# Layernorm, local attention and FFN on one core: when block 3's output turns, three attention pieces and the stacked left rows are issued

## The chip, the core and the metric

The kernel runs on one core of a Trainium2 chip. The metric is the device time of one execution in microseconds. A core has TensorE (PE: matmuls; PEld is the load of the stationary operand), VectorE (DVE), ScalarE (ACT), GpSimd (POOL) and SyncE (SP). Each engine works through its own list of instructions in order, and waits at an instruction until what it depends on has signalled. SP, ACT and POOL issue DMA transfers, each in its own queue; 16 DMA engines serve all queues.

## The reference

With x of 2048 rows and 576 columns:

```
xn  = layernorm(x)
q, k, v = split(xn @ wqkv)                         # 32 heads of 18
at row s, per head: logits over the 8 rows s, s-2, ..., s-14 (rows below 0 masked)
att = softmax(logits * 18**-0.5) @ v of those rows
h   = relu(xn @ w1 + b1) ** 2                      # 4608 columns
out = x + att @ wo + h @ w2 + b2
```

All data are float32.

## The kernel before

**Precision.** Each float32 operand of a matmul is split in two: a high part, which ACT writes as a rounded copy (lines 522 `w1_hi`, 556 `w2_hi`, 998 `o_hi`, 1080 `h_hi`, 1451 `operand_hi`), and a low part, the remainder, which DVE subtracts (`w1_lo`, `w2_lo`, `o_lo`, `h_lo`, `operand_lo`; all record line 128). A product is three matmuls: high by high, high by low, low by high. Names below are of the operand's tile: `w2r` is a raw tile of W2 or the output weights, `w2s` its split; `w1s` split W1; `h` split hidden rows; `q` an attention result.

**Blocks.** The 2048 rows are four blocks of 512 (b = 0 to 3). Blocks 0 and 1 go together first (s = 0), then blocks 2 and 3 (s = 1). For the first FFN matrix, two blocks and two tiles of 128 hidden columns (a pair p, 18 of them) are one 2x2 product of matrices, computed with seven products instead of eight; `ffn_pair` (673) does one pair: seven calls of `product` (691), in the order B11, T1, T2, T3, B21, B22, T4, with relu and square between.

**Left rows.** 576 is 4 times 128 plus 64. The last 64 columns of x and rows of W1 are handled in two ways. In pairs 0 to 2 (`PLAIN` is 3) they are two extra matmuls (`left`, 700). From pair 3 on the seven combinations of these rows are stacked: `ST` holds them for x (`stk` in DRAM, loaded by `load_stack`, 633, into two tiles named `w1r`: places 0 to 3 and 4 to 6, each by two DMAs of 64 partitions), `LW` for W1 (`lw` in DRAM, loaded per pair by `load_left_weights`, 655, into a tile `st`, `mb`, or two tiles `x40`, `x41`, in turn). Then each of the seven products has one more matmul, line 698 with `w1r` as its input.

**Where these loads stand.** `part(i)` (706) is called in each pair after the second product (i = 0), after the sixth (i = 1) and after the seventh (i = 2). In s = 1 it issued, all on SP's queue: at pair 1, i = 0, both `load_stack` (four DMAs); at pair 2, i = 0, `load_left_weights` for pairs 3 and 4; later one pair's `load_left_weights` two pairs ahead. In s = 1 the split W1 of each pair comes back from DRAM in two halves by `w1_again` (535), on ACT's queue, one pair ahead; the half k = 1 holds the slots of B21, B22, T4 and, below pair 3, of the left rows. SP's queue also holds the W2 loads (line 551, issued by `w2_lo`), the stores of finished hidden rows (777) and of operands for the block products (766, 769).

**Attention.** A work item `attention(b, g)` (394) is a generator of 19 pieces for one block and one group of 8 heads, nearly all DVE work: for four row sets a product and a reduction (8 pieces), maximum and subtraction, the exponent (on ACT), normalization, and for four row sets a product and a sum (8 pieces). The last piece stores the result by eight POOL DMAs (line 434). `side(n)` runs the next n pieces; strings of digits say how many at which place.

**The last stages.** After the pairs of s = 1 come the block products for half of the hidden tiles (`phase_blocks`, 1504): 28 steps k, matmuls on line 1514, 12 or 16 to a step; after each step the splits of the operands for step k + 2, weights by the list `WHEN`, and `side(int(LAST[k]))`. Then `phase_b1` (1597) adds the other hidden tiles of block 3: 18 tiles m, 14 matmuls each (line 590), each with one `w2_hi` and `w2_lo` (for the tile two ahead), on even m also an `h_hi` and `h_lo`, and `side(int(SINGLES[m]))`. At m = 12 the attention of block 3 must be complete; `regroup` (982) gathers its rows from DRAM into `st` and `r4` (POOL, line 994). From them `o_hi` turns one column group c of 128 (DVE transpose, line 1011) and splits it (ACT, line 1012), and `o_lo` makes the low part. These stood at m = 14 to 17 for c = 0 to 3 and inside the projection for c = 4. The projection is the loop over five column groups c (`o_ops`) at the end of `phase_b1`; `tail` follows. ACT and DVE keep the order of the code, so what stands behind an `o_hi` waits with it.

Of the kernel before, what the change touches and what calls it, by code (L numbers as in the profile page):

```python
# [9 lines left out]
F32R = mybir.dt.float32r  # L10
# [6 lines left out]
P = 128  # L17
S, D, F = 2048, 576, 4608
H, DH, W, DIL = 32, 18, 8, 2
TB = 512  # L20
NB = S // TB
NJ = TB // P
NC = 5
NF = F // P
NP = NF // 2
# [18 lines left out]
PLAIN = 3  # L44
# [1 line left out]
PIECES = (0, 0, 0, 2, 3, 4, 0, 3, 2, 0, 2, 2, 1, 0, 2, 2, 4, 5)  # L46
SPOTS = ('000001',) + ('110022', '110023', '110023', '110023') * 4 + ('110021',)
QUADS = ('01111110111110', '10100010101011', '00110111111111', '10010000111111', '00000000000001', '00110010101010')
LAST = '0000000000000000001111111111'
SINGLES = '12121212121200000000'  # L50
PAIRED = tuple(range(1, 16, 2))
SINGLE = tuple(p for p in range(NP) if p not in PAIRED)
# [7 lines left out]
def block_kernel(ctx: ExitStack, tc: tile.TileContext, x, xt, wqkv, wo, w1, b1, w2, b2, w1l, w2q, w2l, out):  # L60
# [3 lines left out]
    sb = ctx.enter_context(tc.tile_pool(name="sb", bufs=1))  # L64
# [62 lines left out]
    def tt(out, a, b, op):  # L127
        return nc.vector.tensor_tensor(out=out, in0=a, in1=b, op=op)  # L128
# [18 lines left out]
    def four(dt=F32):  # L147
        return sb.tile([P, 2, TB], dt, name="r4", bufs=4)
# [23 lines left out]
    def load_two_rows(b, h):  # L172
        rows_of.setdefault(b, {})
        t = sb.tile([P, 2, D], F32, name="st")
        for j in range(2):
            rows_of[b][2 * h + j] = t[:, j:j + 1]
        nc.gpsimd.dma_start(t, xv[b, :, 2 * h:2 * h + 2])
# [422 lines left out]
    def dims(t, off, *ap):  # L600
        a = t[tuple(slice(0, 1) for _ in t.shape)]
        return bass.AP(tensor=a.tensor, offset=a.offset + off, ap=[*ap])
# [16 lines left out]
    def left_x(s):  # L619
        v = rv.pop(s)  # L620
        x = lambda k: v[:, STACK[k]]
        tt(x(T3), x(B11), x(T1), ALU.subtract)
        tt(x(T1), x(T1), x(T4), ALU.add)
        tt(x(T2), x(T1), x(B11), ALU.subtract)
        tt(x(B22), x(B21), x(T2), ALU.subtract)

        def store(k, part):
            for i in range(NS):
                nc.gpsimd.dma_start(dims(stscr[s], k * NS * TB + i * TB, [2 * NS * TB, L], [1, TB]), part[:, i])

        yield from high_low(v, store)

    def load_stack(s, t, i):
        n = min(t.shape[1], NS - i)
        for h in range(2):
            nc.sync.dma_start(t[2 * h * L:2 * (h + 1) * L, :n].bitcast(F32), stscr[s][:, i:i + n])
        for k, place in STACK.items():
            if i <= place < i + n:
                ST[k] = t[:, place - i]

    def load_left_w(i, v):
        rv["w", i] = v
        nc.sync.dma_start(v[:, :4], w1l[i])
# [11 lines left out]
    def load_left_weights(s, p):  # L655
        place = (p - PLAIN) % 2 + 1 if not s else (p - PLAIN) % 3
        tiles = ([sb.tile([P, 2 * NS * P], F32R, name="st")[:, :NS * P].rearrange("p (s c) -> p s c", c=P)] if place == 0 else
                 [sb.tile([P, NS, P], F32R, name="mb")] if place == 1 else
                 [mt.tile([P, 4, P], F32R, name="x40"), mt.tile([P, 4, P], F32R, name="x41")])
        i = 0  # L660
        for t in tiles:
            n = min(t.shape[1], NS - i)
            nc.sync.dma_start(t[:, :n].rearrange("p s c -> p (s c)").bitcast(F32),
                              dims(lwscr[p // G], p % G * 2 * L * NS * P + i * P, [NS * P, 2 * L], [0, 2], [1, n * P]))
            for k, place in STACK.items():
                if i <= place < i + n:
                    LW[p % 3, k] = t[:, place - i]
            i += n
# [4 lines left out]
    def ffn_pair(s, p, work, first=False):  # L673
# [32 lines left out]
        def part(i):  # L706

            if not s and (p, i) in ROWS:
                b, h = ROWS[p, i]
                if h:  # L710
                    next(rv["m", b])
                else:
                    rv["m", b] = statistics(b)
                if h < 2:
                    load_two_rows(b, h)
            if i == 0 and not s and p + 1 >= PLAIN and not last:
                load_left_weights(s, p + 1)
            if i == 0 and s:
                for q in range(PLAIN if p + 1 == PLAIN else p + 2, min(p + 3, NP) if p + 1 >= PLAIN else 0):
                    load_left_weights(s, q)  # L720
            if i == 0 and p == 1 and s:
                for q in (0, 4):
                    load_stack(1, sb.tile([P, 4, TB], F32R, name="w1r", bufs=2), q)
            if i == 2 and p == PLAIN - 1 and not s:
                load_stack(0, mt.tile([P, 1, TB], F32R, name="x4d"), 6)
            if s:
                return
            if (p, i) == (0, 1):
                rv["x of"] = left_x(0)
            if (p, i) in ((0, 1), (1, 0)):  # L730
                for _ in range(1 + p):
                    next(rv["x of"])
            if (p, i) == (1, 2):
                load_stack(0, sb.tile([P, 5, TB], F32R, name="kv", bufs=3), 0)
                load_stack(0, sb.tile([P, 1, TB], F32R, name="xf"), 5)
            r = p // G + 1
            if i == 1 and p % G == 1 and G * r < NP:
                load_left_w(r, sb.tile([P, 2 * NS, P], F32, name="st"))
            elif p % G == 2 and G * r < NP:
                if i == 0:  # L740
                    rv["of", r] = left_w(r)
                next(rv["of", r])
# [255 lines left out]
    def o_hi(b, c):  # L998
        if c == NC - 1 and b == 1:
            ot[b, c // 2] = sb.tile([P, 1, 1, TB], F32R, name="xf")  # L1000
        elif c % 2 == 0:
            ot[b, c // 2] = mt.tile([P, 2, 2, TB], F32R, name="h" if b == 1 else "w1s", bufs=3)
        hi = ot[b, c // 2][:, c % 2, 0]
        if c < NC - 1:
            if b != 1:
                of[b, c] = four()[:, 0]
            elif c % 2 == 0:
                t = four()
                of[b, c], of[b, c + 1] = t[:, 0], t[:, 1]
            src = ob[b, 0][:, :, c * L:(c + 1) * L] if c < 3 else ob[b, 1][:, :, :L]  # L1010
            nc.vector.transpose(of[b, c].rearrange("p (u f) -> p u f", f=L), src)
            nc.scalar.activation(hi, of[b, c], AF.Copy)
            return
        t = of[b, c] = four()
        n = L // 2
        nc.vector.transpose(t[:, 0].rearrange("p (u k f) -> p u k f", k=2, f=n),
                            ob[b, 1][:, :, None, OB - n:].to_broadcast([P, NJ * G, 2, n]))
        nc.scalar.activation(t[:, 1].bitcast(F32R), t[:, 0], AF.Copy)

    def o_lo(b, c):  # L1020
        hi = ot[b, c // 2][:, c % 2, 0]
        t = of.pop((b, c))
        if c < NC - 1:
            tt(ot[b, c // 2][:, c % 2, 1], t, hi.bitcast(F32), ALU.subtract)
            return
        nc.vector.tensor_scalar(out=t[:, 0], in0=t[:, 0], scalar1=flip[:, 0:1], scalar2=None, op0=ALU.mult)
        nc.vector.scalar_tensor_tensor(out=hi, in0=t[:, 1], scalar=flip[:, 1:2], in1=t[:, 0],
                                       op0=ALU.mult, op1=ALU.add)
# [475 lines left out]
    def phase_blocks():  # L1504
# [28 lines left out]
        for k in range(len(ORDER)):  # L1533
# [54 lines left out]
            if k == 25:  # L1588
                load_h(1, SINGLE[1])
                h_hi(1, SINGLE[0])  # L1590
                h_lo(1, SINGLE[0])
            side(int(LAST[k]))
        load_h(1, SINGLE[2])
# [3 lines left out]
    def phase_b1():  # L1597
        b = 3
        phase_blocks()
        m = 0  # L1600
        for j, p in enumerate(SINGLE[:-1]):
            for f in range(2):
                w2_hi()
                if f == 0:
                    h_hi(1, SINGLE[j + 1])
                add(b, tile_products(b, 2 * p + f, hs[1, p]))
                w2_lo()
                if f == 0:
                    h_lo(1, SINGLE[j + 1])
                elif j + 3 < len(SINGLE):  # L1610
                    load_h(1, SINGLE[j + 3])
                if len(xr[b]) < 2 and (m == 12 or not queue and current[0] is None):
                    complete(b)
                    regroup(b, 0)
                    regroup(b, 1)
                    open_left(b)
                    load_left(b)
                for c in {14: (0,), 15: (1,), 16: (2,), 17: (3,)}.get(m, ()):
                    o_hi(b, c)
                    o_lo(b, c)  # L1620
                side(int(SINGLES[m]))
                m += 1
        for c in range(NC):
            w2_hi()
            add(b, o_ops(b, c), (NC - 2,) if c == NC - 1 else ())
            w2_lo()
            if c == 1:
                o_hi(b, NC - 1)
                o_lo(b, NC - 1)
        tail()  # L1630

    def tail():
# [396 lines left out]
    phase_a(0, filler)  # L2029
    phase_a(1, phase_b0())  # L2030
    phase_b1()


# [58 lines left out]
```

## Time and profile before

| | us |
|---|---|
| median of 3 runs | 1110.2 |
| lowest, highest | 1109.54, 1112.1 |
| the profiled execution | 1111.5 |
| its span, first to last instruction | 1109.8 |
| PE idle inside the span (1109.8 - 1088.1) | 21.7 |

The times are of whole executions. The profile is one other execution, and its own time lies 1.7 us above its span. "Busy" is time in which an engine had an instruction in work; matmuls overlap, so a busy PE may still run slowly when the granted clock (PEclk, 1.00 is full) is low. "Chain" is the order of work that ended last, followed back from the end. A row such as `x14 [5.61 <-ACT w2s L562]` says that 14 instructions of a kind follow one another, and that their engine was idle for 5.61 us before, until ACT's work on `w2s` at line 562 ended. Times in rows are counted from the span's start. `SPq` and `ACTq` are DMA issues in the queues of SP and ACT.

### The profile page before, as it was taken

The page shows a single profiled execution, that of the slowest core. Times are in us where ns is not written, and L with a number is a line of the kernel's source. Part 1 is how long each engine was busy: PE and PEld are TensorE (multiplying, and loading weights), DVE is VectorE, ACT ScalarE, POOL GpSimd, SP SyncE. Part 2 cuts the span into 40 slices and gives each one's busy share as a digit, 9 for nine tenths or more (in the row PEclk, how much of TensorE's full clock was granted, in tenths as well). Part 3 has the DMA queues.
Part 4 walks back from the last instruction along what each step waited for, and adds up shares of the span by engine and source line. Part 5 has one row for each costly group of instructions (what it writes and reads, how often), then busy time and mean ns, then how long its engine had stood idle before and what let it go on. Part 6 is the DMA issues. An engine that isn't in the chain of part 4 may idle for free.

```text
span 1109.8 us, 13933 instructions
## 1 busy us (share of the span) xinstructions
PE 1088.1 (98%) x4871; PEld 911.2 (82%) x4871; DVE 931.4 (84%) x1245; ACT 570.9 (51%) x800; POOL 160.3 (14%) x294
## 2 busy tenths in 40 slices
PE   9999999999999999999999998999999999999978
PEld 7998888888888888888899877888788788887867
DVE  7967899999998979989998676879789887878955
ACT  5556665666566554555353443555554565533422
POOL 5011220212130100012012201112012030000010
PEclk9999999999999999999999998999999999999999
DMA  8759997898897797876866989998798897664752
GB/s 285 250 196 319 301 394 279 312 372 281 319 340 295 247 370 259 276 240 237 300 184 208 391 252 336 341 376 317 300 384 312 328 348 245 210 200 137 251 178 92
DMA packets 106886, 312.53 MB, mean 282 GB/s; under 512 B 12864, under 2 KB 39488, under 8 KB 95168
## 3 DMA queue, kind: packets, MB, share of 16 engines
q1 hardware_dynamic: 70048, 198.75, 50.9%
q0 software_dynamic: 15584, 71.96, 17.8%
q10 hardware_dynamic: 21184, 40.94, 10.9%
q8 instruction: 38, 0.62, 0.2%
q14 instruction: 32, 0.26, 0.1%
HBM read 216.62 MB, written 94.98 MB: 281 GB/s over the span
## 4 chain that ended last, share of the span: by engine, by line
PE 80%; DVE 10%; DMA 5%; issue 3%; ACT 1%; POOL 0%; SPq 0%; ACTq 0%; DVEq 0%; POOLq 0%
PE p L698 32%; PE p L590 29%; PE p L1187 7%; PE p L1514 6%; DVE pr L128 4%; PE p L1843 2%; DVE h L128 2%; PE p L1191 1%; DMA w1s<-w 1%; DVE w2s L128 1%; PE p L1898 1%; DMA op<-h 1%; PE p L704 1%; DMA out<-h 1%; PE p L1753 1%
## 5 line engine op out<-in xcount | busy, mean ns | idle before, releaser
L590 PE MATMUL p<-h,w2s 128*128 128x512 f32 x1618 | 392.6, 392 | 5.6 <-ACT w2s L562 5.6
L590 PEld LDWEIGHTS p<-h,w2s 128*128 128x128 f32 x1618 | 305.8, 189 | 71.2 <-ACT w2s L562 6.0
L698 PE MATMUL p<-X,w1s 128*128 128x512 f32 x864 | 219.9, 390 | 1.5 <-DVE r L128 1.5
L698 PEld LDWEIGHTS p<-X,w1s 128*128 128x128 f32 x864 | 162.4, 188 | 36.0 <-DVE r L128 1.9
L698 PE MATMUL p<-S,w1s 128*128 128x512 f32 x648 | 167.3, 394 | 0.9 <-ACT p L786 0.9
L698 PEld LDWEIGHTS p<-S,w1s 128*128 128x128 f32 x648 | 121.0, 189 | 30.0 <-ACT r L806 2.9
L562 ACT ACTIVATE w2s<-w2r 128x640 fp32r<-128x640 f32 x132 | 96.7, 734 | 87.9 <-PE p L590 61.8
L434 POOL DMA_DIRECT2D o<-q x128 | 69.5, 620 | 471.6 <-DVE q L128 471.1
L128 DVE TENSOR_TENSOR w2s<-w2r,w2s 128x576 fp32r<-128x576 f32 (+1 forms) x133 | 99.7, 750 | 15.5 <-ACT w2s L562 15.5
L745 ACT ACTIVATE r<-r,b1t 128x512 f32<-128x512 f32 x72 | 52.1, 724 | 116.4 <-DVE r L128 113.6
L128 DVE TENSOR_TENSOR h<-h 128x1024 fp32r<-128x1024 f32 (+1 forms) x74 | 72.6, 989 | 23.2 <-ACT h L762 13.7
L128 DVE TENSOR_TENSOR pr<-lg,kv 128x1152 f32<-128x1152 f32 x64 | 86.7, 1355 | 1.3
L128 DVE TENSOR_TENSOR pr<-q,kv 128x1152 f32<-128x1152 f32 x64 | 86.7, 1354 | 1.1
L128 DVE TENSOR_TENSOR r<-p,r 128x512 f32<-128x512 f32 (+2 forms) x81 | 55.0, 681 | 38.4 <-ACT r L831 20.3
L405 DVE TENSOR_REDUCE lg<-pr 128x64 f32<-128x1152 f32 x64 | 86.4, 1350 | 1.0
L128 DVE TENSOR_TENSOR pr<-pr 128x576 f32<-128x576 f32 (+1 forms) x128 | 77.5, 606 | 3.1
L753 ACT ACTIVATE r<-r 128x1024 f32<-128x1024 f32 x56 | 59.2, 1057 | 0.9
L806 ACT ACTIVATE r<-p 128x512 f32<-128x512 f32 x36 | 21.6, 599 | 57.2 <-PE p L698 57.1
L128 DVE TENSOR_TENSOR w1s<-w1r,w1s 128x1024 fp32r<-128x1024 f32 (+2 forms) x42 | 46.2, 1102 | 5.6 <-ACT w1s L523 5.0
L831 ACT ACTIVATE r<-p 128x512 f32<-128x512 f32 x36 | 21.6, 600 | 56.4 <-PE p L698 56.4
L745 ACT ACTIVATE r<-p,b1t 128x512 f32<-128x512 f32 x72 | 48.2, 671 | 0.0
L128 DVE TENSOR_TENSOR h<-r,h 128x1024 fp32r<-128x1024 f32 (+2 forms) x35 | 39.9, 1146 | 7.6 <-ACT r L753 6.0
(263 smaller groups left out, 1489.8 us busy)
## 6 DMA issues: line engine op xcount, KB each, us to landing
kv<-kvq POOLq DMA_DIRECT2D x32, 1296.0 KB, 9.3
w2r<-in_w SPq DMA_DIRECT2D x112, 320.0 KB, 4.5
w<-w1s SPq DMA_DIRECT2D x21, 1024.0 KB, 7.6
w1s<-w ACTq DMA_DIRECT2D x19, 1024.0 KB, 8.2
h<-r SPq DMA_DIRECT2D x28, 512.0 KB, 6.2
h<-h SPq DMA_DIRECT2D x28, 512.0 KB, 4.3
w<-w1s SPq DMA_DIRECT2D x15, 768.0 KB, 9.1
w1s<-w ACTq DMA_DIRECT2D x15, 768.0 KB, 7.0
```

The costliest lines, as they stand in the source:

```text
L128: return nc.vector.tensor_tensor(out=out, in0=a, in1=b, op=op)
L405: nc.vector.tensor_reduce(out=lg[:, j * HG:(j + 1) * HG].rearrange("p a w -> p w a"), in_=pr.rearrange("p w (a d) -> p w a d", d=DH), axis ...
L434: nc.gpsimd.dma_start(rows[:, i], q[i * L:(i + 1) * L, :, a:z])
L562: nc.scalar.activation(w2s[stream[i]][:, :DE], raw2[i], AF.Copy)
L590: nc.tensor.matmul(yp[b][c], v, a, start=c not in yb[b], stop=c in last and c not in [o[0] for o in ops[i + 1:]], skip_group_check=True)
L698: nc.tensor.matmul(to, l, r, start=start and i == 0, stop=i == len(mm) - 1, skip_group_check=True)
L745: nc.scalar.activation(to, a, AF.Relu, bias=b1t[:, f:f + 1])
L753: nc.scalar.activation(r, r, AF.Square)
L806: nc.scalar.activation(u[:, 0], bb, AF.Copy)
L1187: nc.tensor.matmul(to, l[:, js], r, start=start and n == 0, stop=n == len(mm) - 1, skip_group_check=True)
L1514: nc.tensor.matmul(p, l, r, start=id(p) not in begun, stop=stop, skip_group_check=True)
L1843: nc.tensor.matmul(p[:, :QW], l, r, start=k == 0, stop=k == len(mm) - 1)
```

## The change

It has three parts. The digits of `LAST` place attention pieces at steps 13, 14 and 15 of the block products, none at 19 and 21, and one each at 18, 20 and 22 to 27: eleven pieces, before ten at 18 to 27. The left rows' loads of s = 1 are divided: the first half of the stacked x rows is loaded at pair 1, i = 1, the second half at pair 2, i = 0; the left weights for pair 3 at pair 2, i = 0, those for pair 4 at pair 2, i = 2. And block 3's turns for c = 0 and 1 stand at m = 16 and 17, those for c = 2, 3 and 4 in the projection, behind products 0, 1 and 2.

```diff
-LAST = '0000000000000000001111111111'
+LAST = '0000000000000111001010111111'
...
-            if i == 0 and s:
-                for q in range(PLAIN if p + 1 == PLAIN else p + 2, min(p + 3, NP) if p + 1 >= PLAIN else 0):
-                    load_left_weights(s, q)
-            if i == 0 and p == 1 and s:
-                for q in (0, 4):
-                    load_stack(1, sb.tile([P, 4, TB], F32R, name="w1r", bufs=2), q)
+            if i == 0 and s and p + 1 == PLAIN:
+                load_left_weights(s, PLAIN)
+            if i == (2 if p + 1 == PLAIN else 0) and s and PLAIN <= p + 1 and p + 2 < NP:
+                load_left_weights(s, p + 2)
+            if i == 2 - p and p in (1, 2) and s:
+                load_stack(1, sb.tile([P, 4, TB], F32R, name="w1r", bufs=2), 4 * p - 4)
...
-                for c in {14: (0,), 15: (1,), 16: (2,), 17: (3,)}.get(m, ()):
+                for c in {16: (0,), 17: (1,)}.get(m, ()):
                     o_hi(b, c)
                     o_lo(b, c)
...
-            if c == 1:
-                o_hi(b, NC - 1)
-                o_lo(b, NC - 1)
+            if c < 3:
+                o_hi(b, c + 2)
+                o_lo(b, c + 2)
```

## The prediction

> **What bounds the kernel now.** I read the page first, then the waits of PE, the chain of waits, the windows, and the timelines of three places. The page says that PE is the bound and has little left to give:
>
> ```profile
> PE 1088.1 (98%) x4871; PEld 911.2 (82%) x4871; DVE 931.4 (84%) x1245; ACT 570.9 (51%) x800; POOL 160.3 (14%) x294
> ```
>
> The waits of PE (engine and line, what it waited for, total us, times, longest) name all of it. These are five of eight rows:
>
> ```profile
> PE p L590 <- ACT w2s L562: 5.6, 1, 5.6
> PE p L704 <- DMA w1s<-w: 5.5, 1, 5.5
> PE p L698 <- DVE r L128: 1.5, 1, 1.5
> PE p L1514 <- DVE h L128: 1.4, 1, 1.4
> PE p L1514 <- DVE w1s L128: 0.8, 2, 0.4
> ```
>
> Two waits carry 11.1 us, and the change stands at both. The first is in pair 2 of blocks 2 and 3 (s=1). The chain of waits there (start, us, what):
>
> ```profile
> 646.05 8.40 DMA out<-h
> ...
> 654.53 14.67 DMA w1s<-w
> ...
> 669.24 1.22 PE p L704 x2
> 670.46 1.71 PE p L590 x4
> 672.17 4.12 PE p L698 x12
> ...
> 676.75 1.59 PE p L590 x7
> ```
>
> PE wanted the second half of pair 2's W1 at 669.24 - 5.5 = 663.74 and had it at 669.20. A wait of this length costs more than itself: the last row is 1.59/7 = 0.227 us a matmul, while the 2 + 4 + 12 matmuls that come first took 672.17 + 4.12 - 669.24 = 7.05 us in place of 4.09. The granted clock shows why:
>
> ```profile
> 670.00:672.00 2.00, 2.00 (x7) 1.52 (x6) 0.00 (x0) 0.00 (x0) 0.00 (x0) 0.50 1.00 398
> ```
>
> So this place costs 5.5 + 2.96 = 8.5 us. The second is at block 3's output projection:
>
> ```profile
> 1064.10 0.31 DVE L128 TENSOR_TENSOR q<-pr 128x144 f32<-128x144 f32 x1
> 1064.69 4.33 POOL L434 DMA_DIRECT2D o<-q  x8 [35.66 <-DVE q L128]
> 1072.44 0.56 POOL L994 DMA_DIRECT2D st<-o  x1 [3.42 <-DMA o<-q]
> 1077.08 0.71 DVE L1011 STREAM_TRANSPOSE r<-st 128x512 f32<-128x512 f32 x1 [10.09 <-DMA st<-o]
> 1077.82 0.63 ACT L1012 ACTIVATE w1s<-r 128x512 fp32r<-128x512 f32 x1 [12.09 <-DVE r L1011]
> 1078.36 0.72 ACT L562 ACTIVATE w2s<-w2r 128x640 fp32r<-128x640 f32 x1
> 1079.13 5.98 PE L590 MATMUL p<-h,w2s 128*128 128x512 f32 x14 [5.61 <-ACT w2s L562]
> 1081.06 0.72 ACT L562 ACTIVATE w2s<-w2r 128x640 fp32r<-128x640 f32 x1
> 1084.95 7.23 PE L590 MATMUL p<-w1s,w2s 128*128 128x512 f32 x31
> ```
>
> The last attention result leaves DVE at 1064.41; stores, gather and landing bring the regrouped rows at 1077.05, 12.6 us later. The turn of column group 0 (o_hi, called at m=14) waits for them on DVE, its split behind it on ACT, and behind that the W2 split for tile 17, which needs none of this. PE stops at 1079.13 - 5.61 = 1073.52 with tile 17 (14 matmuls, 3.18 us at full rate) still to do. The first output product starts at 1084.95 instead of 1076.70: 8.25 us lost.
>
> **The change, part by part.**
>
> *Loads.* No byte is removed. In SP's order the four stack loads go from the start of pair 1 to its third product (two) and the start of pair 2 (two), and LW4 behind pair 2's operand stores and W2 load. DVE's split that frees w2r in pair 1, and SP's queue before:
>
> ```profile
> 649.11 0.75 DVE L128 TENSOR_TENSOR w2s<-w2r,w2s 128x576 fp32r<-128x576 f32 x1
> ```
> ```profile
> 649.38 4.25 SPq L636 DMA_DIRECT2D w1r<-stk  x4
> 654.71 0.34 SPq L551 DMA_DIRECT2D w2r<-in_w  x1
> 655.18 0.55 SPq L663 DMA_DIRECT2D st<-lw  x1
> 656.53 0.54 SPq L663 DMA_DIRECT2D mb<-lw  x1
> ```
>
> SP is not tied to PE: it issued pair 2's loads at 655.18 and 656.53, 7 us before PE wanted that pair's W1. So the two steps are no two times; what changes is the queue's order: w2r (issued as DVE ends its split at 649.86), first stack half (1024 KB), st, second half (768 KB). The landing of the last stack load (KB, us from issue) and the rate (last column, GB/s):
>
> ```profile
> w1r<-stk SPq DMA_DIRECT2D x1, 384.0 KB, 16.2
> ```
> ```profile
> 654.00:656.00 2.00, 2.00 (x10) 1.65 (x10) 1.88 (x4) 1.10 (x2) 0.00 (x0) 1.00 1.16 438
> 656.00:658.00 2.00, 2.00 (x11) 1.65 (x10) 1.47 (x2) 0.93 (x2) 0.00 (x0) 1.00 1.02 225
> ```
>
> From 656 the rate is halved, while the stack rows move (64 partitions to a DMA); the last of the four, issued at about 653.2, lands at 669.4, together with W1. Estimate: by 656.5 W1 had about 0.28 MB of its 1.05 MB (half of 438 GB/s for 1.3 us) and got the other 0.77 MB in 12.7 us, 61 GB/s beside 165 GB/s of stack rows. After, w2r comes first: 0.33 MB in 1.6 us at some 200 GB/s each, W1 at 0.60 MB by 658.1. The first stack half then lasts 1.05 MB/165 GB/s = 6.4 us, W1 gets 0.39 MB more, and the rest beside st: landed at 664.8. That leaves PE a wait of 1.1 us. A wait as short as the 1.4 us of L1514 above lowers no clock (its 20 us, clock third from the end):
>
> ```profile
> 1000.00:1020.00 20.00, 18.14 (x77) 13.97 (x77) 16.25 (x20) 7.17 (x8) 0.00 (x0) 1.00 0.51 164
> ```
>
> So the half-rate stretch goes too: 5.5 - 1.1 + 2.96 = **7.4 us**. Bounds: 0 (nothing lands earlier) and 8.5. The trigger at 654.53 follows the landing of block 1's output store (654.45), with which it shares no tile; I take it to be a shared completion counter and leave it; if the reordering frees it, W1 starts earlier and the wait is 0. Next is pair 3: it begins 7 us earlier; st, the first half and pair 3's W1 are then some ten us in the queue, less than the 14.67 and 16.2 us of the crowd before, and LW4 is needed a pair later. I cost these at nothing; if that cover fails, pair 3 waits for up to the 4 to 6 us by which these landings exceed ten.
>
> [...]
>
> *Attention pieces at the blocks.* One piece more (11, was 10); the softmax exponent, its normalization and a product go from steps 18 to 20 to 13 to 15; 19 and 21 are left empty. DVE around them, and the product's group on the page:
>
> ```profile
> 974.85 1.23 DVE L128 TENSOR_TENSOR h<-h 128x1024 fp32r<-128x1024 f32 x1 [1.85 <-ACT h L1453]
> 979.18 1.23 DVE L128 TENSOR_TENSOR S<-X,S 128x1024 fp32r<-128x1024 f32 x1 [3.11 <-ACT S L1437]
> 989.60 1.37 DVE L128 TENSOR_TENSOR S<-p,S 128x512 f32<-128x512 f32 x2 [0.83 <-PE p L1514]
> 992.27 0.40 DVE L416 TENSOR_REDUCE sm<-lg 128x32 f32<-128x256 f32 x1
> 993.44 1.22 DVE L128 TENSOR_TENSOR X<-X 128x1024 f32<-128x1024 f32 x1
> 1000.00 1.25 DVE L128 TENSOR_TENSOR pr<-pr 128x576 f32<-128x576 f32 x2
> 1001.51 1.22 DVE L128 TENSOR_TENSOR X<-X 128x1024 f32<-128x1024 f32 x1
> ```
> ```profile
> L128 DVE TENSOR_TENSOR pr<-lg,kv 128x1152 f32<-128x1152 f32 x64 | 86.7, 1355 | 1.3
> ```
>
> Normalization (992.27 to 993.44, 1.17 us) and product (1.36) fit into 1.85 + 3.11 us of idle time; without that cover they cost up to 2.5. A sum (1000.00 to 1001.51) now stands at step 18, 0.83 of it hidden in idle time. Up to step 21 the operand splits come 1.17 - 0.68 = 0.5 us earlier, from 22 on 2.0. That removes waits of 0.4 and 1.4 and leaves some 0.4 later: 1.8 by this count, **1.5 us** taken, since a DVE running full has shifts I cannot see. Bounds: -2.5 and 2.2 (all waits of L1514).
>
> *Turns.* Same 5 turns, splits and corrections; they stand two m later, then one product later each. ACT's split for tile 17 is no longer behind a turn, so PE runs through tile 17. What is late next is the first turn: attention's end plus 12.6, plus 0.71 + 0.63 and the gaps, 1.45 us. In this stage DVE is full; of its work, one piece (a product, 1.36) has gone to the blocks, a W2 split (0.75) and an h split (1.23, like the row of 974.85) now stand behind the last result, and DVE enters up to 1.7 earlier: 5.0 together. Against it, the exponent falls a step earlier on ACT, ahead of a W2 split and an h split that DVE needs (0.72 and about 1): up to 1.7. Attention ends at 1064.41 - 3.2 (of 1.6 to 5.0) = 1061.2, the operand is ready at 1075.3. Tile 17 ends at 1076.7 - 1.5 = 1075.2. I take 0.4 us of wait there: **7.8 us** of 8.25 kept. From then on each product's preparation takes 1081.06 - 1078.36 = 2.70 us against 3.18 us of PE, so it stays hidden.
>
> Sum: 7.4 + 1.5 + 7.8 = 16.7 us. The profiled execution's span is 1109.8 and its time 1111.5, so 1094.8 for such a one; the median shown is 1.3 below that, 1110.2, so **1093.5**.
>
> **The rivals.**
> - *The W1 wait stays.* SP still issues 2.2 MB around ACT's 1 MB. If ACT's load gets the same share whatever SP moves, it lands 14.67 us after its trigger as before, and 9.3 us are left of the sum: 1110.2 - 9.3 = 1100.9; with the wait shortened to 3 us, 1098.4. Against it: the halved rate while stack rows move, and their later place. [...]
> - *The projection still waits.* The regrouped rows come no earlier, as attention is 12.6 us of transfers away: 1078.5 against 1075.2 is 3.3 us, and if the clock halves again 2.6 more: 1093.5 + 5.5 = 1099. For it: DVE is full here, so little slack. Against: the pieces counted above.
> - *Both*: 1104 to 1106.
> - *Slower: the projection becomes a ladder.* If each turn is ready only after the product before it has ended, every one of five products waits its 2.70 us, 13.5 in all, and 65 matmuls at half clock cost 0.2 each, 13 more: 26.5 against the 16.7 won, some 1120. It decides at a preparation cycle above 3.18 us. Against it: the 2.70 us measured with the same instructions.
>
> [...]
>
> **How the numbers follow.** Chances: forecast 0.64 (1090 to 1097); W1 wait stays 0.15; projection waits 0.13; both 0.03; no change to be told 0.02; ladder 0.03. The range goes from 1090 (8.5 + 2.2 + 8.25 = 18.9 won gives 1091.3, and 1.3 is half the spread of the runs shown) to 1101.5, which takes in both single failures. A difference under 0.2% (2.2 us) cannot be told from none: faster 0.95, same 0.02, slower 0.03.
>
> **What would show it.** In pair 2 the row of L704 with its DMA wait is gone or about 1 us, no slice with clock 0.5 follows, and W1 lands near 665. In the block steps the waits of L1514 fall under 1 us in sum. At the projection no w2s wait of L590, 14 matmuls of tile 17 in 3.2 us, and a first turn near 1061.2 + 12.6 - 7.4 = 1066.4. Wrong would be: a W1 landing of 14 us again, a new wait at pair 3's first product, or turns that PE waits for at products 1 to 4.

## The result, and the profile after

| | before | after |
|---|---|---|
| median, us | 1110.66 (4 runs) | 1099.87 (4 runs) |
| lowest, highest | 1109.54, 1112.1 | 1098.53, 1102.08 |
| the profiled execution, its span | 1111.5, 1109.8 | 1099.84, 1098.1 |

The ratio of after to before is 0.9904, with a 95% interval of 0.9884 to 0.9924: 10.8 us faster by the medians. The forecast was 1093.5, a gain of 16.7. The time lies in the range given, which was drawn to take in that rival too, but it lies where the first rival put it (the W1 wait stays: 1098.4 to 1100.9).

The waits of PE in the changed kernel (engine and line, what it waited for, total us, times, longest), four of seven rows:

```profile
PE p L704 <- DMA w1s<-w: 4.0, 1, 4.0
...
PE p L1187 <- DVE h L1063: 2.0, 1, 2.0
PE p L698 <- DVE r L128: 1.5, 1, 1.5
PE p L1514 <- DVE w1s L128: 0.7, 1, 0.7
```

The wait of 5.6 us at line 590 is gone, and of the 2.2 us at line 1514 there is 0.7 left. But the wait for W1 in pair 2, forecast at 1.1, is 4.0. The chain of waits there:

```profile
647.81 7.82 DMA w1s<-w
...
655.71 13.96 DMA w1s<-w
...
669.71 0.72 PE p L704 x2
670.44 1.48 PE p L590 x4
671.91 3.80 PE p L698 x12
```

The half of W1 took 13.96 us to land, before 14.67. The 18 matmuls that follow took 671.91 + 3.80 - 669.71 = 6.0 us in place of 4.09: the clock fell again, to 0.65 and 0.50 in the slices from 670 to 674. So this place costs 4.03 + 1.91 = 5.94 us, before 8.46: **2.5 us** won where 7.4 were forecast. What the DMA engines did meanwhile (the window view: us, then busy time of each engine, then granted clock, DMA share, GB/s):

```profile
658.00:660.00 2.00, 2.00 (x10) 1.65 (x10) 1.53 (x2) 0.77 (x2) 0.00 (x0) 1.00 1.17 233
660.00:662.00 2.00, 2.00 (x11) 1.65 (x10) 1.90 (x4) 1.59 (x2) 0.00 (x0) 1.00 1.03 221
```

And SP's queue in the timeline:

```profile
652.37 1.40 SPq L636 DMA_DIRECT2D w1r<-stk  x2
656.54 0.55 SPq L663 DMA_DIRECT2D st<-lw  x1
657.19 1.20 SPq L636 DMA_DIRECT2D w1r<-stk  x2
```

The second half of the stacked rows goes out at 657.19, 1.5 us after the trigger of W1's half. The two steps lie 4.8 us apart and stand in front of the same 1 MB of W1; the rate falls to 221 as it did before.

The other two parts, from PE's timeline (before, the first and the last row of the block products; after, the same two and the rows that follow):

```profile
925.26 1.52 PE L1514 MATMUL p<-h,S 128*128 128x512 f32 x6
...
1018.96 0.62 PE L1514 MATMUL p<-w1s,r 128*128 128x512 f32 x2
```
```profile
924.06 1.52 PE L1514 MATMUL p<-h,S 128*128 128x512 f32 x6
...
1015.55 0.62 PE L1514 MATMUL p<-w1s,r 128*128 128x512 f32 x2
1016.00 57.28 PE L590 MATMUL p<-h,w2s 128*128 128x512 f32 x252
1073.17 15.07 PE L590 MATMUL p<-w1s,w2s 128*128 128x512 f32 x65
```

The blocks took 93.70 us and take 91.49: **2.2 us** won, 1.5 forecast. From there to the end of the span it was 1109.8 - 1018.96 = 90.84 and is 1098.1 - 1015.55 = 82.55: **8.3 us** won, 7.8 forecast. PE runs 252 matmuls in a stretch up to tile 17, and the 65 of the projection follow with no gap.

Sum of the three: 13.0. The spans differ by 11.7. What is missing is the wait of 2.0 at line 1187, at 541 us, where before had 0.2; no instruction up to there was changed, and in the eleven timed kernels below PE waits between nothing and 1.3 at that line. The 0.5 us that are left lie between pair 3 and the blocks; some 0.4 of them are a wait of line 698 for ACT's work on `p` (line 786), which came twice before (0.9 us in sum) and once after (0.5).

### The profile page after: what moved, and what is told of

Same layout as the page of the kernel before. It is cut to its first block, busy times and chain, and to the rows that moved or that the text cites. A ratio compares the mean times of both kernels' runs of the same rounds, so it can differ in the third digit from the quotient of the medians.

```text
span 1098.1 us, 13935 instructions
## 1 busy us (share of the span) xinstructions
PE 1083.5 (99%) x4871; PEld 908.9 (83%) x4871; DVE 930.9 (85%) x1245; ACT 570.7 (52%) x800; POOL 160.0 (15%) x294
## 4 chain that ended last, share of the span: by engine, by line
PE 90%; DVE 5%; DMA 3%; issue 1%; ACT 1%; POOL 0%; ACTq 0%; DVEq 0%; POOLq 0%
PE p L590 35%; PE p L698 34%; PE p L1187 9%; PE p L1514 6%; PE p L1843 2%; DMA w1s<-w 2%; PE p L1191 2%; DVE pr L128 1%; PE p L1898 1%; PE p L704 1%; DMA w2r<-in_wo 1%; DVE h L128 1%; PE p L1753 1%; DVE w2s L128 0%; DVE r L128 0%
```

## The experiments

The theories for the missing 4.9 us. **A, narrow rows:** the stacked x rows, 64 partitions to a DMA, move at half rate (225 GB/s after 438 in the kernel before, 221 and 233 above), and W1 has to go through with them wherever SP's queue has them in these 12 us. **B, late trigger:** the traces have the landings of SP's and ACT's transfers on eight completion counters, which the program deals out, and the trigger of W1's half came 0.08 us after the transfer before it on its counter had landed. In the kernel before that is block 1's output store (landed 654.45, trigger 654.53). In the changed kernel it is W1's own first half, which ends at 655.63, and the trigger follows at 655.71, though ACT's copy of PE's product, behind which it stands, ended at 654.31. **C, equal share:** ACT's queue gets its part of the engines whatever SP moves.

All runs, each beside the kernel before on its chip (1110.66 in the first five rows, 1111.19 in the next four, 1110.03 in the last three):

| | median, us | ratio to before, 95% | PE's W1 wait in pair 2 |
|---|---|---|---|
| the change | 1099.87 | 0.9904 [0.9884, 0.9924] | 4.0 |
| e1_loads | 1109.31 | 0.9985 [0.9972, 0.9999] | 3.4 |
| e4_early | 1102.75 | 0.9916 [0.9892, 0.9941] | none, 7.2 elsewhere |
| e5_wide | 1094.59 | 0.9847 [0.9824, 0.9869] | 0.5 |
| e6_lane | 1097.68 | 0.9893 [0.9863, 0.9922] | 1.9 |
| e2_last | 1105.57 | 0.9943 [0.9931, 0.9955] | 5.3 |
| e3_turns | 1106.48 | 0.9950 [0.9935, 0.9965] | 5.4 |
| e7_wide_alone | 1104.69 | 0.9937 [0.9924, 0.9950] | 1.3 |
| e8_wide_old_order | 1096.70 | 0.9867 [0.9852, 0.9883] | 0.9 |
| e9_two_copies_narrow | 1100.44 | 0.9910 [0.9895, 0.9924] | 3.9 |
| e11_wide_again | 1094.15 | 0.9851 [0.9835, 0.9868] | none |
| e12_wide_old_again | 1095.88 | 0.9868 [0.9849, 0.9888] | 2.3 |

(e10_ports, one execution of 1119.3 us, is a measurement of single transfers.)

### The loads alone

The edit is the diff's part in `part(i)`, on the kernel before.

> The kernel before with the loads' part of the change alone. Theory A (narrow rows): the second half of pair 2's W1 comes late because the stacked x rows, 64 partitions to a DMA, move at half rate (225 GB/s where they run, 420 to 438 just before) in the same 16 engines, and the change leaves them beside W1; so the part is worth what the traces show at that place, 8.46 - 5.94 = 2.5 us: 1108.1, with a wait of PE at line 704 of about 4 us and half clock after it. The prediction's term: 7.4 us, 1103.3, wait about 1 us. Equal share (the two queues split the engines whatever SP moves): 0, 1110.6.

1109.31, a gain of 1.4 us. The waits show 3.4 at line 704 in place of 5.5, with the half clock after it (0.50 from 670 to 672; its landing took 13.55 us). By the interval this part alone was worth 0.1 to 3.1 us, far from 7.4.

### Wide rows

```diff
-    stscr = [dram.tile([2 * L, NS, TB], F32, name=f"stk{s}") for s in range(2)]
+    stscr = [dram.tile([2 * (s + 1) * L, NS, TB], F32, name=f"stk{s}") for s in range(2)]
...
-                nc.gpsimd.dma_start(dims(stscr[s], k * NS * TB + i * TB, [2 * NS * TB, L], [1, TB]), part[:, i])
+                for h in range(s + 1):
+                    nc.gpsimd.dma_start(dims(stscr[s], (h * 2 * L + k) * NS * TB + i * TB, [2 * NS * TB, L], [1, TB]), part[:, i])
...
+            if s:
+                nc.sync.dma_start(t[:, :n].bitcast(F32), stscr[s][:, i:i + n])
+                break
```

> The changed kernel with the stacked x rows of s = 1 held twice in DRAM, so that each of the two loads is one DMA of 128 partitions in place of two of 64, at the same places in SP's queue; POOL issues 14 more stores for it earlier. The trigger of the W1 half is not freed. Theory A (narrow rows): the slices after 656 run at 400 GB/s or more in place of 213 to 233, W1's half lands by 664, no wait at line 704: 1094.0. Theory B (late trigger) and theory C (equal share): trigger at 655.7 and landing 13 to 14 us later as before: 1099.9.

1094.59, 5.3 us less than the changed kernel, and within 1.1 of the forecast made for that one. The same bytes stand at the same places, and the trigger still waits for its first half: it goes 1.6 us after ACT's copy begins, in the changed kernel 2.0. The chain and the windows of this kernel:

```profile
653.14 10.89 DMA w1s<-w
...
664.08 0.72 PE p L708 x2
664.80 0.93 PE p L590 x4
665.73 2.74 PE p L702 x12
```
```profile
658.00:660.00 2.00, 2.00 (x11) 1.65 (x10) 1.82 (x4) 1.46 (x2) 0.00 (x0) 1.00 0.94 389
660.00:662.00 2.00, 2.00 (x10) 1.69 (x9) 0.17 (x1) 1.75 (x3) 0.00 (x0) 1.00 1.00 411
```

Where the changed kernel has 233 and 221 GB/s stand 389 and 411, W1 lands in 10.89 us, PE waits 0.5 and keeps its clock (18 matmuls in 4.39 us). A holds; B and C, which left 1099.9 here, fall as the main cause.

> The changed kernel with the stacked x rows of s = 1 held twice in DRAM, as in e5_wide, but loaded as before by two DMAs of 64 partitions, each from its own copy. Theory A (narrow rows): the width at the destination counts, so nothing is won: 1099.9, 213 to 233 GB/s after 656, a wait of about 4 at line 704. If instead it was the second reading of the same DRAM rows that was slow: as e5_wide, 1094.6, 390 GB/s or more.

```diff
-            nc.sync.dma_start(t[2 * h * L:2 * (h + 1) * L, :n].bitcast(F32), stscr[s][:, i:i + n])
+            nc.sync.dma_start(t[2 * h * L:2 * (h + 1) * L, :n].bitcast(F32), stscr[s][2 * s * h * L:][:2 * L, i:i + n])
```

1100.44, with the wait of 3.9 back and 13.00 us of landing. Beside e11_wide_again, on the same chip, it is 6.3 us slower. One of its windows:

```profile
660.00:662.00 2.00, 2.00 (x10) 1.65 (x10) 0.82 (x3) 1.21 (x3) 0.00 (x0) 1.00 1.06 221
```

So it is neither the second copy, nor POOL's 14 more stores, nor reading one DRAM row twice. What is left is the shape of the loads: two DMAs of 64 partitions, each on one side, in place of one over all 128. The next run tells whether it is the number of partitions or which ones.

> e5_wide with eight loads added at the start of the tail, where the queues are quiet, one after the other into a dead tile, 8 KB to a partition: partitions 0 to 63, 32 to 95, 64 to 127, 0 to 127, 32 to 63, 32 to 95, 0 to 63, 0 to 127. The output stores stand behind them, so the time of the kernel grows by some 15 us and says nothing. Theory P (it matters which partitions): 32 to 95 takes less than 0 to 63 though both move 512 KB, by about 0.5 MB x (1/225 - 1/430 GB/s) = 1.1 us; 32 to 63, a quarter of the bytes of 0 to 127, takes about half of its transfer time, 1.2 us beside 2.4. Theory N (the number of partitions): 32 to 95 takes as long as 0 to 63, about as long as 0 to 127, which moves twice as much.

```diff
+        t, v = sb.tile([P, 4, TB], F32R, name="w1r", bufs=2), stscr[1]
+        nc.sync.dma_start(t[:64].bitcast(F32), v[:64, :4])
+        nc.sync.dma_start(t[32:96].bitcast(F32), v[32:96, :4])
...
```

In SP's timeline each load goes out when the one before has landed (the first landed 5.4 us after 1075.86, the second went out at 1081.24), so the difference of two starts is its time:

```profile
1075.86 0.48 SPq L1639 DMA_DIRECT2D w1r<-stk  x1
1081.24 0.53 SPq L1640 DMA_DIRECT2D w1r<-stk  x1
1085.20 0.46 SPq L1641 DMA_DIRECT2D w1r<-stk  x1
1090.04 0.34 SPq L1642 DMA_DIRECT2D w1r<-stk  x1
1095.04 0.34 SPq L1643 DMA_DIRECT2D w1r<-stk  x1
1098.08 0.52 SPq L1644 DMA_DIRECT2D w1r<-stk  x1
1102.08 0.45 SPq L1645 DMA_DIRECT2D w1r<-stk  x1
1107.07 0.34 SPq L1646 DMA_DIRECT2D w1r<-stk  x1
```

Partitions 0 to 63: 5.4 and 5.0 us; 64 to 127: 4.8; 32 to 95: 4.0 and 4.0; all 128, twice the bytes: 5.0; 32 to 63, a quarter of them: 3.0. The eighth load, all 128 again, took 6.1 us with the output stores issued behind it. Here it mattered which partitions: the same 512 KB took 0.8 to 1.4 us less when they straddled the middle (1.1 expected), and 1 MB over all 128 (5.0 us) took no longer than 512 KB on one side of it (4.8 to 5.4). What makes the difference is not shown. The gain of 32 to 95 is in part unexplained too: it puts 256 KB on each side, which 32 to 63 alone had landed in 3.0 us, and takes 4.0. Where the other 1.0 us goes is not shown. The prediction saw the row (225 GB/s) and wrote the cause beside it, in brackets, but did not ask what it would take to lift it.

### Trigger, place, order

> The changed kernel with pair 0's hidden rows of s = 1 stored from POOL's queue in place of SP's (line 777, one DMA of 512 KB). By the program's dealing of completion counters the trigger of pair 2's second W1 half then follows the first store of block 1's rows (issued at 646.8, landed about 650.6) and not its own first half (landed 655.6): it can go at 653.7, behind ACT's copy. The stacked rows stay where they are. Theory A (narrow rows): the landing moves with the trigger at most, to 667.7, a wait of 2.0 to 3.5: 1096 to 1098.5. Theory B (late trigger): it lands 8 to 9 us after 653.7, no wait: 1094.0. Theory C (equal share): 667.7, 1096.

```diff
-            nc.sync.dma_start(hscr[s][p], r1.rearrange("p f t -> p (f t)"))
+            (nc.gpsimd if s and not p else nc.sync).dma_start(hscr[s][p], r1.rearrange("p f t -> p (f t)"))
```

```profile
652.28 0.01 ACT r L831
652.28 13.81 DMA w1s<-w
...
666.14 0.73 PE p L704 x2
```

The trigger is freed: it goes with ACT's copy, at 652.28. The transfer takes 13.81 us all the same, the wait is 1.9, and this time no half clock follows (1.00 from 664 to 672). That is close to A's 2.0 (which C shares) and not B's none. So the counter cost about 2 us of start here, and not the length of the transfer. By this profile the place costs 1.9 us in place of 5.94, because the shorter wait leaves the clock alone: the late trigger is a second cause of the missing 4.9 us, small in landing time, but enough to bring the half clock. The time, 1097.68, is spread from 1096.49 to 1105.17; three of six runs lie at 1096.5 to 1096.8. The profiled one took 1102.05 and has a new wait of 4.7 us at 701.6, behind a store issued at 680.22 that took 20.64 us to land. Why that store is late in some executions was not tried.

> The changed kernel with both halves of the stacked x rows loaded in pair 0, near 638 to 641 us, where SP is idle and the DMA rate falls from 407 to 87 GB/s. The count of earlier transfers changes with it, so the trigger of pair 2's second W1 half no longer waits for its first half. Theory A (narrow rows) and theory B (late trigger, the only cause): landing within 9 us of the trigger, no wait at line 704, 5.9 us less than the changed kernel: 1094.0. Theory C (equal share): 13.96 us after a trigger at 653.7, landing at 667.7, a wait of 2.0 with no half clock: 1096. If the rows get in the way of pair 0's W2 tiles instead, PE waits there and the time is 1098 or more.

```diff
-            if i == 2 - p and p in (1, 2) and s:
-                load_stack(1, sb.tile([P, 4, TB], F32R, name="w1r", bufs=2), 4 * p - 4)
...
                 nc.sync.dma_start(kept(b, NC - 1), yleft)
+                for q in (0, 4):
+                    load_stack(1, sb.tile([P, 4, TB], F32R, name="w1r", bufs=2), q)
```

1102.75, against 1094.0 by A and B: only the last clause of the expectation came true. A window at the end of the stacked rows, then the chain:

```profile
650.00:652.00 2.00, 1.32 (x6) 0.75 (x4) 0.99 (x3) 0.00 (x0) 0.00 (x0) 1.00 1.02 241
```
```profile
643.67 13.49 DMA w2r<-in_w
...
658.52 4.48 PE p L698 x12
```

The gap in the DMA rate for which they were meant is over when pair 0's W2 tiles are due, and the narrow rows run on at 208 to 241 GB/s until 652. A W2 tile of 320 KB behind them landed after 13.49 us, its split on ACT held the copy that PE needed, and PE waited 7.2 us. The W1 wait had only moved to another transfer.

> The kernel before with the stacked x rows held twice in DRAM and loaded by DMAs of 128 partitions (as in e5_wide), and no part of the change. Theory A (narrow rows): the second half of pair 2's W1 lands in time though all four loads stand in their old places; the wait of 5.5 at line 704 and its half clock (2.96) go: 1102.2. If the order in SP's queue matters beside the width, a wait of 1 to 3 us stays: 1105. Theory C (equal share): 1110.7.

1104.69, 6.5 us less than before, with no part of the change. The W1 wait is 1.3 us and lowers no clock (1.00 from 664 to 672), so 8.46 - 1.3 = 7.2 are won at the place: nearly the 7.4 that the prediction had given to the division of the loads. The time is the second of the two that A allowed (1105, with a wait of 1 to 3 us from the order of the queue), not the first.

> e5_wide with the loads' part of the change undone: wide rows, the old order in SP's queue, new LAST and new turns. Theory A (narrow rows): the order is worth nothing once the rows are wide: 1094.6, as e5_wide. If the division in two steps is worth its 2.5 us by itself: 1097.

> e5_wide once more, on the same chip as e12_wide_old_again, to tell whether the division of the loads is worth anything once the rows are wide (1094.6 against 1096.7 on two chips, intervals overlapping). Theory A: the two are the same within 1 us, 1094.5 to 1097 both. If the division counts by itself: this one lower by 2 us or more.

> e8_wide_old_order once more beside e11_wide_again: wide rows, the old order in SP's queue, new LAST and new turns. Theory A: as e11_wide_again within 1 us. If the division counts by itself: 2 us or more above it, with a wait at the place of line 704 above 1 us.

1096.70 against e5_wide's 1094.59, and on one chip 1095.88 against 1094.15: twice the same sign, 1.7 to 2.1 us, with intervals that overlap. Once the rows are wide the division is worth perhaps 2 us or nothing; this stays open. PE's W1 wait was 0.9, 1.3 and 2.3 us in the three kernels with wide rows in the old order, and 0.5 or none in the two with the new. Part of it is the clock (last section): the profiled execution of e12_wide_old_again, the slowest of its four with 1098.52, waited 2.3 us and then ran at half clock. Where the wait could come from is seen in the chain of e12_wide_old_again: in the old order the counter falls to another neighbour, a store, which landed at 657.51, and the trigger came at 657.53.

```profile
648.57 8.94 DMA out<-r
657.53 9.70 DMA w1s<-w
```

### Pieces and turns

> The kernel before with the new LAST alone. Theory S (the pieces serve two places): the waits of line 1514 fall from 2.2 to 0.7 us and the attention of block 3 ends some 2.5 us earlier after the blocks' end, as in the changed kernel (42.5 against 45.0 us), so the wait of tile 17 falls from 5.6 to about 3.1: 1110.7 - 2.2 - 2.5 = 1106, or 1103.4 if the half clock after it goes too. Rival (the pieces serve the blocks alone, the turns the projection): the wait of tile 17 stays at 5.6: 1108.4.

> The kernel before with the new places of block 3's turns alone. Theory S: tile 17 no longer waits, but the attention ends as late as before, so the first turn's operand is ready at about 1078.5 and PE wants it at 1076.7: a wait of about 2 us at line 590 on the turn's split, 8.25 - 2 = 6.3 won: 1104.4. Rival (turns alone): no wait at the projection, 8.25 won: 1102.4. Theory L (a ladder of turns): each of five products waits, 1120.

1105.57, where S had 1106, and 1106.48, 2.1 us above the 1104.4 that S had. The profiled execution of e3_turns is a quick one (1103.84, with six from 1103.01 to 1107.9), so its waits do not account for the median. The waits of PE, first with the new `LAST` alone, then with the new turns alone:

```profile
PE p L590 <- ACT w2s L562: 2.9, 2, 2.8
...
PE p L1514 <- DVE w1s L128: 0.7, 1, 0.7
```
```profile
PE p L590 <- ACT w1s L1012: 1.8, 1, 1.8
```

With `LAST` alone the blocks take 91.48 us, as after the whole change (2.2 won), and the wait of tile 17 is halved: the pieces act at both places. With the turns alone the blocks are as before (93.67), tile 17 runs through, and the first product waits 1.8 us for its turn, where the expectation had about 2. From the blocks' end to the span's end `LAST` wins 4.9 us, the turns 6.4, both together 8.3: each covers part of the same 8.25.

## Why the prediction was right and wrong

**The loads, 7.4 forecast, 2.5 measured: the step that failed.** It is the estimate of what W1's half gets: 0.28 MB by 656.5 before, and with the division 0.60 MB by 658.1 and the rest beside `st`, landed at 664.8. It landed at 669.67. The half of the rate that it gives W1 from its trigger on was the author's estimate, and no run shows it there. (PE wanted it at 665.68 in this execution, 1.9 us later than in the profile before, so the wait is 4.0 where 1.1 was forecast.) The DMA section from W1's trigger on, before (654.5 to 660) and after (655.7 to 660.3; queue: packets, MB, share of 16 engines), has one queue only, SP's:

```profile
q1 hardware_dynamic: 281, 1.52, 104.8%
```
```profile
q1 hardware_dynamic: 447, 1.49, 108.7%
```

For 5.5 and 4.6 us after its trigger no byte of W1 moved, while 1.5 MB of SP's went; the division took next to nothing of that away. Then W1 ran beside the narrow rows. The prediction itself had said that SP is not tied to PE, so that two steps are no two times, and it drew the wrong sum from that: all bytes stayed within 12 us of W1's trigger, and the 64 partitions to a DMA, with which they moved at 221 and 233 GB/s, were not touched by the change. e5_wide and e9_two_copies_narrow show the second with the same bytes at the same places: 389 and 411 GB/s and 1094.59 us with 128 partitions, 215 and 221 GB/s and 1100.44 us with 64. Why W1's first byte waits so long is not shown. The prediction had named a W1 landing of 14 us as a sign of being wrong, and it was 13.96. The bound of 0 to 8.5 held, and the rival (the wait stays, 1098.4 to 1100.9) is what came.

The other half of that step, "I take it to be a shared completion counter and leave it", was right in kind: e6_lane took the counter away and the trigger went 2 us sooner by PE's work. It did not shorten the transfer, so it is not the main cause; but leaving it cost the half clock as well.

**The equal share** that this rival assumed got the size of the term nearly right for another reason. The DMA section of e5_wide from the trigger to 656.5, and from there to 660.3, where W1's half was ACT's only load in flight (q10 is ACT's by its bytes):

```profile
q1 hardware_dynamic: 499, 1.46, 106.7%
```
```profile
q1 hardware_dynamic: 90, 0.71, 51.8%
q10 hardware_dynamic: 92, 0.75, 48.7%
```

Here too nothing of W1 moved for 3.4 us. Then ACT's queue got 0.75 of 1.46 MB, one half. (The prediction's 61 GB/s for W1 beside 165 is an average over 12.7 us before; W1 moved in the last 9.1 of them.) In the changed kernel it got 0.22 of 0.39 MB from 660.3 to 662, before its next load went out at 662.49. That is about the equal share; the 3.4 us before it do not follow from one. So an equal share and narrow rows are no rivals: once it moved, W1 got about half of what moved, and the narrow rows lowered what moved, to 221 and 233 GB/s from 389 and 411.

**The block steps, 1.5 forecast, 2.2 measured.** The mechanism was right: the waits of line 1514 fell from 2.2 to 0.7 us, by the 1.5 forecast, though 0.7 is left where some 0.4 was expected. The rest of the 2.2 is not in the list of waits. In part it is that this wait cost more between two starts than its idle time: before, one matmul started at 1002.10 and the next at 1003.92, 1.82 us in place of 0.23, for a wait of 1.43. **The projection, 7.8 forecast, 8.3 measured.** Right, and in its parts: e3_turns shows the late first turn without the pieces (1.8 us), e2_last what the pieces bring to the attention's end. The 0.4 us of wait that the sum took for the first turn is not there: its split ended on ACT at 1073.11, and PE's products go on at 1073.17. That is close: of the nine profiles with the new pieces and turns, five have no wait there and four have 0.2 to 0.8 us (e10_ports, e6_lane, e8_wide_old_order, e4_early), so the 0.4 was a fair guess. The preparation of a product, 2.70 us against 3.18, stayed hidden, so there was no ladder.

**Of the sum**, 16.7 became 13.0 in the profiled spans, less 1.8 at line 1187, which varies from one execution to the next and which the prediction took to be fixed. With wide rows the change gives 1094.15 to 1094.59, within 1.1 us of the forecast. That is luck: the kernel differs in the shape of its loads, and the width does there the work that the prediction gave to the division (7.2 of 7.4 by e7_wide_alone). The range held for a like reason: its upper end had been set to take in this very failure.

## What to carry to other kernels

Which partitions a load writes set its time here: 512 KB took 4.0 us over partitions 32 to 95 and 4.8 to 5.4 over 0 to 63 or 64 to 127 (e10_ports), and the slices with the stacked rows went from 221 and 233 GB/s to 389 and 411 with 128 partitions to a DMA. So look for slices with all DMA engines busy and half the GB/s of their neighbours, and widen those loads before moving them about. Moving loads in the order of SP's queue, which ran some 7 us ahead of PE, won 1.4 us of the 7.4 forecast by itself (e1_loads); ask when a load will be issued, what the queues have issued before it, and what else is then in flight. When two edits mend one wait, do each alone: their gains here (4.9 and 6.4) do not add up (8.3).

## What the runs showed of the hardware

**Half clock followed idle time within a stretch of 3.41 us, not the length of a wait.** The prediction quotes no wait between 1.5 and 5.5 us. Two windows, of e12_wide_old_again after a wait of 2.33 us, and of e2_last after one of 2.75:

```profile
668.00:670.00 2.00, 2.00 (x6) 1.54 (x6) 1.24 (x3) 0.00 (x0) 0.00 (x0) 0.56 1.03 428
```
```profile
1076.00:1078.00 2.00, 2.00 (x10) 1.64 (x9) 1.30 (x3) 1.23 (x3) 0.00 (x0) 1.00 0.39 110
```

The granted clock (third number from the end) is lower after the shorter one and not after the longer. The traces record when it changes. In the kernel before it was half from 668.14 to 674.97 and from 1077.74 to 1084.57, in the changed kernel from 670.60 to 674.01: 6.83, 6.83 and 3.41 us, twice and once 3.41, and the 402.77 us between the first two are 118 times that. Laid on this grid, PE was idle for all 3.41 us of the stretch ahead of each of these two, and for 2.53 us ahead of the one in the changed kernel (667.19 to 670.60). By the windows e1_loads fell to half at 669.72, after a stretch with 2.25 us of idle time, and e12 at 668.22, with its whole wait of 2.33 in the stretch from 664.81. The least that half clock followed is 2.16 us, at the end of the kernel before (1105.05 to 1108.46). The most that it did not follow is 1.68 in the traces of the two kernels (540.89 to 544.31, changed kernel), and e6_lane's wait of 1.89 kept full clock too. Half clock went on for another stretch where its own had 1.10 and 1.39 us of idle time (before), and ended where it had none (before and after): so the same place cost 2.96 us beside the wait before, and 1.91 after. That e2's wait of 2.75 was cut in two by the grid is an estimate from this: either part would be under 2.16 us if the cut fell more than 0.59 us from both its ends; where the grid lies in e2_last is not shown. Another estimate from these numbers: a wait of under 1.9 us does not lower the clock by itself, one of over 4.3 (twice 2.16) does, and between them it is a matter of where the wait falls.

**When a transfer ended depended on its neighbours more than on its own start.** W1's half took 13.00 to 14.67 us in five kernels with narrow rows beside it (14.67 before, 13.96 after, 13.81 e6_lane, 13.55 e1_loads, 13.00 e9_two_copies_narrow) and 8.99 to 10.89 us in four with wide ones (10.89 e5_wide, 9.70 e12_wide_old_again, 9.08 e7_wide_alone, 8.99 e8_wide_old_order), with triggers between 652.28 and 657.61. The last of these triggers, 657.61 in e7_wide_alone, had its half landed at 666.69; in the kernel before, where it came at 654.53, that was 669.20.
